# One chunk's direct term added by GpSimd, and the second block's first products recorded behind the first norm

## The chip, the core and the metric

The kernel runs on one core of a Trainium2 chip. A core has a matrix engine (PE, with PEld for its weight loads), a vector engine (DVE), a scalar engine (ACT), GpSimd (POOL) and a queue engine (SP) that issues most transfers. The metric is the time of one execution in microseconds, and lower is better. Three runs of the kernel before took 1164.25, 1165.2 and 1166.44 us, median 1165.2. The execution that the profiler recorded took 1164.2 us; its span from the first to the last instruction is 1162.0 us.

## The reference

Four layers follow each other on a signal of 2048 positions by 512 channels: a state-space convolution, a gated feed-forward network, and both again, each behind a layer norm and each added to its input.

```python
x = A_u
for _ in range(2):
    x = x + _A_ref(_layernorm(x), ...)   # y = irfft(rfft(u) * rfft(K)) + u * Dskip
    x = x + _B_ref(_layernorm(x), ...)   # (silu(x @ w_gate) * (x @ w_up)) @ w_down
```

K is a filter of 2048 taps for each channel, summed from 128 complex exponentials. The convolution is causal. Dskip, the direct term, multiplies the normed input; adding Dskip to the first tap of K has the same effect.

## The kernel before

The positions are cut into four blocks of 512 (`T`), and the convolution into products of block spectra. A block's output is the sum, over the blocks up to it, of an input spectrum times a filter spectrum. The channels are cut into eight chunks of 64 for the filter and into two halves (`h`) for the convolution; the spectra are cut into four quarters `q`, taken in the order 0, 3, 1, 2.

For each chunk the kernel makes the taps on PE (`lags`), spreads them over the partitions into `kt`, adds the direct term to the first tap (`skip`, L503) and turns `kt` into filter spectra on PE. For the last chunk the spreading goes through PE (`spread_pe`: matmuls L523, then one ACT copy L525 into `kt`). `first_parts` (L580) and `later_parts` (L531, with ACT copies L598 and L599 and a DVE addition L600 per quarter) make its spectra.

`ssm_half` convolves one half of one block. For each quarter it multiplies the input spectrum by the filter spectrum on DVE (L776, a tile `yk` of 128x1024); for an earlier block it loads a filter tile `w` and an input tile `uu`, multiplies (L776 into `t`) and adds (L779). Two DVE operations fold `yk` into `yf` (L781, L782), PE transforms it back (L796 into `pi`), and ACT or DVE combines the quarters (L748, L756, L757). After four quarters DVE combines them into the block's rows in two pieces (L811 to L815, then L820 to L825). The first block's two halves are the generators `conv[0]` and `conv[1]`; its input spectra and filter spectra are in SBUF, while each later block also needs loads.

The feed-forward weights are stored as pairs of 16-bit parts. `split_weights` loads them in pieces; ACT makes the high part (`hi`, L664 and L689) and DVE the low part (`lo`, L669 and L692). The scale of these splits comes from `scales()`, a run of small DVE operations (L344 to L356), so that no split can start before it. `first_norm` makes the norm of the first 256 rows for the feed-forward network: DVE statistics (L203 to L205), a power on POOL (L206), DVE L209, ACT rows L841, PE transposes L843, ACT L846 and DVE L848. `sizes` (ACT L607) and `direct_size` (ACT L192, DVE L193) bound the values for a later scale.

What sets the order: up to L1213 the instructions of ACT, DVE, PE and POOL stand as the code records them (`tc.manual_schedule`), and `take(generator, n)` records the next `n` steps of one part. SP and everything behind that block are ordered by a scheduler, which can also put later instructions into gaps of the recorded order. Each engine and each queue runs its instructions in order; an instruction that waits holds up all behind it.

The piece that the change touches, L1161 to L1212, runs from about 250 to 318 us of the span: the first block's convolution, the last chunk's spectra, the weight splits and the first norm, up to the first feed-forward matmul (`pgu`, L909, L910 and L912). From there on the feed-forward networks of the blocks alternate on PE with the convolutions of the next ones; `pgu` has two buffers, and each is freed by a DVE operation on it (L916).

Of the kernel before, what the change touches and what calls it, by code (L numbers as in the profile page):

```python
# [21 lines left out]
L, D, F = 2048, 512, 1376  # L22
# [22 lines left out]
SEQ = ((0, 0), (0, 1), (0, 2), (1, 0), (0, 3), (1, 1), (1, 2), (1, 3))  # L45
# [29 lines left out]
def kernel(ctx, tc, x, a_re, a_im, b_re, b_im, c_re, c_im, log_dt, d_skip,  # L75
                           w_gate, w_up, w_down, c_ef, c_ei, c_ek, c_am, c_eh, c_eih, out):
    nc = tc.nc
    V, A, G, PE = nc.vector, nc.scalar, nc.gpsimd, nc.tensor
# [9 lines left out]
    def tl(shape, name, tag, dt=F32):  # L88
        return sb.tile(shape, dt, name=name, tag=tag, bufs=BUFS[tag])
# [4 lines left out]
    def psml(shape, name):  # L94
        return ps.tile(shape, F32, name=name, tag="sml", bufs=4)
# [92 lines left out]

    def direct_size():

        da = tl([1, D], "da", "uu")
        A.activation(da, dsk, AF.Abs)  # L192
        V.tensor_reduce(dmax, da, axis=AX.X, op=OP.max)  # L193

# [32 lines left out]
    def stt(o, i0, s, i1, op1):  # L227
        V.scalar_tensor_tensor(o, i0, s, i1, OP.mult, op1)  # L228

    def load_x(xt, layer, b):  # L230
        if layer == 0:
            nc.sync.dma_start(xt, x[0, b * T:(b + 1) * T, :].rearrange("(c p) d -> p c d", p=P))
        else:
            nc.sync.dma_start(xt, xdr[b].rearrange("c p d -> p c d"))
# [5 lines left out]
    def whole(t):  # L240

        return t.rearrange("p i (c d) -> p i c d", c=NQ)
# [257 lines left out]
    def skip(ch, kt, eng):  # L500

        k = kt[0:1, :, 0]
        eng.tensor_tensor(k, k, dsk[:, ch * DC:(ch + 1) * DC].rearrange("p (g d) -> p g d", g=4), OP.add)  # L503
# [14 lines left out]
    def spread_pe(ks, kt):  # L518

        kp = pbig([P, 4, 16, 16], "kp")  # L520
        for grp in range(4):
            for ga in range(4):
                PE.matmul(kp[32 * ga:32 * ga + 32, grp], lhsT=ident[:, 32 * grp:32 * grp + 32], rhs=ks[:, ga],  # L523
                          start=True, stop=True, tile_position=(0, 32 * ga))
        A.activation(kt, kp, AF.Copy)  # L525
# [79 lines left out]
    def sizes(ch, kt, junk):  # L605

        A.activation(junk, kt, AF.Abs, accum_out=wsum[:, ch:ch + 1])  # L607
# [21 lines left out]
    def take(it, n):  # L629
        for _ in range(n):  # L630
            next(it, None)
# [99 lines left out]
    def ssm(layer, b):  # L731

        if (layer, b) == SEQ[INV]:
            nc.sync.dma_start(eih, c_eih)
        for h in range(2):
            yield from ssm_half(layer, b, h)

    def ssm_half(layer, b, h):
        first = layer == 0 and b == 0
        half = SEQ.index((layer, b)) >= INV  # L740
        hs = slice(h * HD, (h + 1) * HD)
        bb = {}

        def combine(q, pi):
            if q < 2:
                pair = tl([P, 2, 2, HD], "bb", "bd") if h == 0 or not first else bb1[:, q]
                bb[q], bb[q, 1] = pair[:, 0], pair[:, 1]
                A.activation(bb[q], pi, AF.Copy, scale=sy[:, 1:2] if half else 1.0)  # L748
                return
            s = bb[3 - q]  # L750
            bb[q] = bb[3 - q, 1]
            if half:
                stt(bb[q], pi, sy[:, 2:3], s, OP.add)
                stt(s, pi, sy[:, 1:2], s, OP.add)
            else:
                V.tensor_tensor(bb[q], s, pi, OP.subtract)  # L756
                V.tensor_tensor(s, s, pi, OP.add)  # L757

        late = []
        for _ in range(4):  # L760
            hq, q, u = ahead.pop(0)
            nxt = next(spec, None)
            if nxt:
                ahead.append(nxt)
            yk = tl([P, NQ, 2, 2, DC], "yk", "y1")
            y = yc if half else tl([P, 2, HD], "yf", "w")
            for k in range(b + 1):
                if k == 0:
                    w, uu = w0r[:, h, q], u
                else:  # L770
                    w = tl([P, NQ, 2, DC], "w", "w")
                    nc.sync.dma_start(w, wdr[k, h, q])
                    uu = tl([P, NQ, 2, DC], "uu", "uu")
                    nc.sync.dma_start(uu, udr[layer][b - k, h, q])
                t = tl([P, NQ, 2, 2, DC], "t", "t") if k else yk
                V.tensor_tensor(t, uu.unsqueeze(2).to_broadcast([P, NQ, 2, 2, DC]),  # L776
                                w.unsqueeze(3).to_broadcast([P, NQ, 2, 2, DC]), OP.mult)
                if k:
                    V.tensor_tensor(yk, yk, t, OP.add)  # L779
            yo = whole(y)  # L780
            V.tensor_tensor(yo[:, 0], yk[:, :, 0, 0], yk[:, :, 1, 1], OP.subtract)  # L781
            V.tensor_tensor(yo[:, 1], yk[:, :, 0, 1], yk[:, :, 1, 0], OP.add)  # L782
            if half:
                yl = yl2[:, QORD.index(q) % 2]
                A.activation(yl[:, 0], y, AF.Copy, scale=sy[:, 0:1])  # L785
                stt(yl[:, 1], y, sy[:, 0:1], yl[:, 0], OP.subtract)
            pi = psml([P, 2, HD], "pi")
            with tc.high_priority(offset=0 if first else BOOST):
                for o in range(2):
                    if half:  # L790
                        terms = [(eih[:, q, 0 if i == o else 1 + o, le], yl[:, ly, i])
                                 for i in range(2) for le, ly in ((0, 0), (0, 1), (1, 0))]
                    else:
                        terms = [(ei[:, q, 0 if i == o else 1 + o], y[:, i]) for i in range(2)]
                    for k, (e, m) in enumerate(terms):
                        PE.matmul(pi[:, o], lhsT=e, rhs=m, start=k == 0, stop=k == len(terms) - 1)  # L796
            late.append((q, pi))
            if first and q < 2 or len(late) > 1:
                combine(*late.pop(-1 if first and q < 2 else 0))
            yield  # L800
        for l in late:
            combine(*l)
        s03, e03, d03, f03 = bb[0][:, 0], bb[0][:, 1], bb[3][:, 0], bb[3][:, 1]
        s12, e12, d12, f12 = bb[1][:, 0], bb[1][:, 1], bb[2][:, 0], bb[2][:, 1]
        xt = xs[SEQ.index((layer, b)) % 3]
        if h == 0 and not first:
            load_x(xt, layer, b)
        o = [xt[:, c, hs] for c in range(4)]
        t1 = tl([P, HD], "t1", "t1")
        t2 = tl([P, HD], "t2", "t1")  # L810
        V.tensor_tensor(t1, s03, s12, OP.add)  # L811
        stt(t2, d12, TT, e12, OP.subtract)
        V.tensor_tensor(o[0], o[0], t1, OP.add)
        stt(t1, e03, -TT, d03, OP.add)
        V.tensor_tensor(t1, t1, t2, OP.add)  # L815
        stt(o[1], t1, CC, o[1], OP.add)
        yield
        t1 = tl([P, HD], "t1", "t1")
        t2 = tl([P, HD], "t2", "t1")
        V.tensor_tensor(s03, s03, s12, OP.subtract)  # L820
        V.tensor_tensor(f03, f03, f12, OP.add)
        stt(t2, d03, TT, e03, OP.subtract)
        stt(t1, e12, TT, d12, OP.subtract)
        V.tensor_tensor(s03, s03, f03, OP.subtract)
        V.tensor_tensor(t1, t1, t2, OP.add)  # L825
        stt(o[2], s03, HH, o[2], OP.add)
        stt(o[3], t1, CC, o[3], OP.add)
        yield
# [122 lines left out]
    with tc.manual_schedule(engines={mybir.EngineType.Activation, mybir.EngineType.DVE, mybir.EngineType.PE, mybir.EngineType.Pool}):  # L951
# [165 lines left out]
        c, kts, tail = NCH - 1, (kt2[:, 0], kt2[:, 1]), {}  # L1117
# [29 lines left out]
        load_x(xs[0], 0, 0)  # L1147
        split(0, 0, 3)
        conv = [ssm_half(0, 0, h) for h in range(2)]

        def slots():
# [9 lines left out]
        norm = first_norm(tl([P, 2, D], "nn1", "hf"))  # L1161
        take(conv[0], 1)
        spread_pe(ks, kts[1])
        skip(c, kts[1], V)
        take(conv[0], 1)
        scales()
        split(1, 0)
# [20 lines left out]
        split(0, 0, 1)  # L1188
        take(odd, 2)
        take(conv[1], 1)  # L1190
        take(norm, 1)
        take(rest, 2)
        take(odd, 1)
        take(norm, 1)
        take(rest, 1)
        take(odd, 2)
        split(1, 0)
# [10 lines left out]
        take(rest, 4)  # L1208
        split(0, 0, 3)
        sizes(c, kts[1], ks)  # L1210
        direct_size()
        nn2 = tl([P, 2, D], "nn2", "nn")  # L1212
        take(second(*sec[-1]), 2)  # L1213
    pscale = product_scale()
# [7 lines left out]
    xs[2] = tl([P, 4, D], "xf", "xf")  # L1222
    for i, lb in enumerate(SEQ):
        if i + 1 < len(SEQ):
            take(ssm(*SEQ[i + 1]), 100)
        if i == 0:
            take(pscale, 100)
        ffn(*lb, ready if i == 0 else None)
# [38 lines left out]
```

## Time and profile before

| what | us |
|---|---|
| median of three runs | 1165.2 |
| the profiled execution | 1164.2 |
| its span | 1162.0 |
| PE busy | 1100.7 (95%) |
| DVE busy | 998.6 (86%) |
| ACT busy | 598.7 (52%) |
| POOL busy | 107.9 (9%) |

The profile gives for each engine the instructions in order of time, each with the idle time of the engine ahead of it and what ended that wait. Shares over the whole span mix stages with different limits, so the stages are read one by one. Times of day below are microseconds from the start of the span.

### The profile page before, as it was taken

To read this page: it belongs to the slowest core of one execution; us is meant where nothing else is said; L and a number is where in the kernel's file an instruction comes from. 1 tells how busy PE (TensorE), PEld (TensorE's weight loads), DVE (VectorE), ACT (ScalarE), POOL (GpSimd) and SP (SyncE) were. 2 spreads that over 40 slices of the span, in tenths; PEclk is the share of its full clock that TensorE was granted. 3 is DMA by queue.
4 is the path that set the end of the run, shared out by engine and by line. 5 is a ranking of instruction groups with operands and counts; after the bars stand their busy time and mean duration, and the time that the engine had idled before them with its cause. 6 is when DMAs were issued, how large, how long until landed. Compare 5 with 4: busy or idle time off the path is not lost.

```text
span 1162.0 us, 24400 instructions
## 1 busy us (share of the span) xinstructions
PE 1100.7 (95%) x9942; PEld 877.9 (76%) x9942; DVE 998.6 (86%) x1586; ACT 598.7 (52%) x1198; POOL 107.9 (9%) x162
## 2 busy tenths in 40 slices
PE   2989999998889999999999999999999999999998
PEld 1868888877766868687868687868777686876875
DVE  8999999959789899999899999989994999983212
ACT  6989889733553353557453534655433452334211
POOL 0113222210000010010010000210000010000000
PEclk9989999998899999999999999999999999999999
DMA  5357777866383446332254544343534145312000
GB/s 208 131 161 164 169 175 187 197 171 218 122 268 122 132 122 219 101 115 73 79 155 140 126 162 141 105 128 93 158 109 150 48 122 145 115 42 46 15 23 19
DMA packets 127314, 150.38 MB, mean 129 GB/s; under 512 B 50897, under 2 KB 75985, under 8 KB 127202
## 3 DMA queue, kind: packets, MB, share of 16 engines
q1 hardware_dynamic: 115298, 123.32, 34.8%
q0 software_dynamic: 11904, 25.50, 9.5%
q8 instruction: 78, 1.28, 0.5%
q14 instruction: 34, 0.28, 0.1%
HBM read 98.70 MB, written 33.82 MB: 114 GB/s over the span
## 4 chain that ended last, share of the span: by engine, by line
PE 33%; DVE 27%; issue 7%; DMA 4%; ACT 3%; SPq 1%; POOL 1%; DVEq 0%; ACTq 0%; POOLq 0%
PE pgu L909 5%; PE pgu L910 5%; PE pgu L912 5%; DVE t L776 4%; PE py L924 4%; DVE yk L779 4%; PE py L925 4%; PE py L926 3%; DVE yk L776 3%; DVE z L228 2%; PE pi L796 2%; PE pf L280 2%; DVE sg L916 2%; DMA w<-wdr 2%; DMA mix<-nn 2%
## 5 line engine op out<-in xcount | busy, mean ns | idle before, releaser
L909 PE MATMUL pgu<-mix,wsl 128*128 128x256 f16 x1280 | 299.2, 273 | 5.0 <-DVE sg L916 5.0
L910 PE MATMUL pgu<-mix,wsl 128*128 128x256 f16 x1280 | 298.9, 273 | 0.0
L912 PE MATMUL pgu<-mix,wsl 128*128 128x256 f16 x1280 | 195.4, 273 | 0.0
L910 PEld LDWEIGHTS <-wsl 128*128 128x128 f16 x1280 | 125.4, 98 | 21.9 <-issue 5.4
L924 PE MATMUL py<-wsl,hh 128*128 128x512 f16 (+1 forms) x352 | 133.5, 379 | 6.3 <-DVE xg L929 4.2
L909 PEld LDWEIGHTS <-wsl 128*128 128x128 f16 x1280 | 125.4, 98 | 16.2
L912 PEld LDWEIGHTS <-wsl 128*128 128x128 f16 x1280 | 125.4, 98 | 14.9
L926 PE MATMUL py<-wsl,hl 128*128 128x512 f16 (+1 forms) x352 | 133.4, 379 | 1.2 <-DVE hl L918 1.1
L776 DVE TENSOR_TENSOR t<-uu,w 128x1024 f32<-128x1024 f32 x96 | 116.7, 1215 | 5.5 <-DMA w<-wdr 5.2
L925 PE MATMUL py<-wsl,hh 128*128 128x512 f16 x320 | 121.3, 379 | 0.0
L915 ACT ACTIVATE sg<-pgu,sc 128x512 f32<-128x512 f32 x80 | 54.6, 683 | 126.6 <-PE pgu L912 122.0
L779 DVE TENSOR_TENSOR yk<-yk,t 128x1024 f32<-128x1024 f32 x96 | 116.6, 1214 | 0.1
L916 DVE SCALAR_TENSOR_TENSOR sg<-pgu,sc,sg 128x512 f32<-128x512 f32 x80 | 59.4, 743 | 52.2 <-ACT sg L915 52.0
L917 ACT ACTIVATE hh<-sg 128x512 f16<-128x512 f32 x80 | 50.1, 626 | 82.3 <-DVE sg L916 82.3
L531 PE MATMUL pw<-kt,ek 128*128 128x256 f32 (+1 forms) x384 | 92.2, 377 | 0.0
L531 PEld LDWEIGHTS pw<-kt,ek 128*128 128x128 f32 x384 | 73.5, 196 | 8.7
L796 PE MATMUL pi<-yl,mix 128*128 128x256 f16 x576 | 78.9, 273 | 1.3 <-ACT yl L785 0.9
L280 PE MATMUL pf<-z,eh 128*128 128x256 f16 x576 | 74.9, 272 | 0.6 <-DVE z L228 0.6
L776 DVE TENSOR_TENSOR yk<-u,w0r 128x1024 f32<-128x1024 f32 x56 | 68.0, 1214 | 0.8 <-ACT u L282 0.8
L918 DVE TENSOR_TENSOR hl<-sg,hh 128x512 f16<-128x512 f32 x80 | 54.7, 683 | 15.5 <-ACT hh L917 15.5
L496 PE MATMUL pk<-re,g 128*32 128x64 f32 x1024 | 65.1, 317 | 2.6 <-DMA g<-g 1.9
L925 PEld LDWEIGHTS <-hh 128*128 128x128 f16 (+1 forms) x352 | 34.5, 98 | 42.5 <-issue 7.0
(237 smaller groups left out, 2160.5 us busy)
## 6 DMA issues: line engine op xcount, KB each, us to landing
w<-wdr SPq DMA_DIRECT2D x96, 256.0 KB, 2.8
uu<-udr SPq DMA_DIRECT2D x96, 256.0 KB, 3.0
udr<-u POOLq DMA_DIRECT2D x32, 256.0 KB, 2.6
g<-g POOLq DMA_DIRECT2D x6, 1024.0 KB, 9.1
udr<-u SPq DMA_DIRECT2D x16, 256.0 KB, 2.9
n<-xdr SPq DMA_DIRECT2D x4, 1024.0 KB, 5.7
kdr<-ks SPq DMA_DIRECT2D x6, 512.0 KB, 2.6
kt<-kdr SPq DMA_DIRECT2D x24, 128.0 KB, 3.0
```

Source lines behind the costliest of these rows:

```text
L280: PE.matmul(pf[:, o], lhsT=e, rhs=m, start=k == 0, stop=k == len(terms) - 1)
L531: PE.matmul(pw[:, i], lhsT=e, rhs=kt[:, :, c + 4 * k0:4 * k1:4, :].rearrange("p g k d -> p k g d"), start=c == 0, stop=c == 3)
L776: V.tensor_tensor(t, uu.unsqueeze(2).to_broadcast([P, NQ, 2, 2, DC]), w.unsqueeze(3).to_broadcast([P, NQ, 2, 2, DC]), OP.mult)
L779: V.tensor_tensor(yk, yk, t, OP.add)
L796: PE.matmul(pi[:, o], lhsT=e, rhs=m, start=k == 0, stop=k == len(terms) - 1)
L909: PE.matmul(o, lhsT=wgu(wi, k, 0)[:, fs], rhs=nh[:, k], start=k == 0, stop=False)
L910: PE.matmul(o, lhsT=wgu(wi, k, 1)[:, fs], rhs=nh[:, k], start=False, stop=False)
L912: PE.matmul(o, lhsT=wgu(wi, k, 0)[:, fs], rhs=nlo[:, k], start=False, stop=k == 3)
L916: V.scalar_tensor_tensor(sg, pgu[:, 1], sc6[:, 4:5], sg, OP.mult, OP.mult)
L924: PE.matmul(py[:, r], lhsT=hh[:n, f, rc], rhs=wd(f, 0)[:n], start=f == 0, stop=False)
L925: PE.matmul(py[:, r], lhsT=hh[:n, f, rc], rhs=wd(f, 1)[:n], start=False, stop=False)
L926: PE.matmul(py[:, r], lhsT=hl[:n, f, rc], rhs=wd(f, 0)[:n], start=False, stop=f == FT - 1)
```

## The change

Three edits. The last chunk's `skip` is given to GpSimd. The size of the direct term is recorded some steps earlier, with its tile in another pool. The first quarter of block 1 (its products, up to the folded `yf`) is recorded behind the second step of the first norm; for that `ssm_half` yields once more in that quarter, and the generator is finished where the whole of it stood.

```diff
-        da = tl([1, D], "da", "uu")
+        da = tl([1, D], "da", "sg")
...
-        for _ in range(4):
+        for s in range(4):
...
             V.tensor_tensor(yo[:, 1], yk[:, :, 0, 1], yk[:, :, 1, 0], OP.add)
+            if (layer, b, h, s) == (0, 1, 0, 0):
+                yield
...
-        skip(c, kts[1], V)
+        skip(c, kts[1], G)
...
         take(conv[1], 1)
+        direct_size()
+        block1 = ssm(0, 1)
         take(norm, 1)
         take(rest, 2)
         take(odd, 1)
         take(norm, 1)
+        take(block1, 1)
         take(rest, 1)
...
         sizes(c, kts[1], ks)
-        direct_size()
...
-            take(ssm(*SEQ[i + 1]), 100)
+            take(ssm(*SEQ[i + 1]) if i else block1, 100)
```

The lines behind the new ones move down in the changed kernel: L796 becomes L798, L820 becomes L822, L848 becomes L850, L909 becomes L911.

DVE ahead of and behind the last chunk's direct term, before (`kt` holds its taps, `yk` and `yf` are the first block's products):

```order
L776 TENSOR_TENSOR yk<-mix,w0r 128x1024
L781 TENSOR_TENSOR yf<-yk 128x256
L782 TENSOR_TENSOR yf<-yk 128x256
L503 TENSOR_TENSOR kt_429<-kt_429,tdk 1x4x16
L776 TENSOR_TENSOR yk<-mix,w0r 128x1024
L781 TENSOR_TENSOR yf<-yk 128x256
L782 TENSOR_TENSOR yf<-yk 128x256
L344 TENSOR_REDUCE c_2718<-cmx 128x3
```

On DVE L503 is gone and the rest stands as it stood. It now stands on POOL, behind the last accumulating stores of the filter and ahead of the first norm's power:

```order
L327 DMA st<-in_B_w_up_dram 128x344 x6
L538 DMA wdr<-wa 128x3x128 x2
L503 TENSOR_TENSOR kt_429<-kt_429,tdk 1x4x16
L206 TENSOR_TENSOR rs<-rs,mhalf 128x2
L223 TENSOR_TENSOR rs<-mv,mhalf 128x2
```

POOL has one instruction more there, and L206 comes behind it. DVE around the first norm, before:

```order
L205 TENSOR_SCALAR rs<-mv 128x2
L669 SCALAR_TENSOR_TENSOR wsl_2665<-st_2758,sc_92,wsl_2665 128x2x344
L669 SCALAR_TENSOR_TENSOR wsl_2666<-st_2758,sc_92,wsl_2665 128x2x344
L209 SCALAR_TENSOR_TENSOR rs<-mv,rs 128x2
L600 TENSOR_TENSOR wos<-pw,wos 128x2x3x64 x2
L600 TENSOR_TENSOR mix<-pw,mix 128x2x3x64
L848 TENSOR_TENSOR mix<-pt,mix 128x1024
```

The same place in the changed kernel:

```order
L209 SCALAR_TENSOR_TENSOR rs<-mv,rs 128x2
L600 TENSOR_TENSOR wos<-pw,wos 128x2x3x64
L776 TENSOR_TENSOR yk<-u,w0r 128x1024
L776 TENSOR_TENSOR t<-uu,w 128x1024
L779 TENSOR_TENSOR yk<-yk,t 128x1024
L781 TENSOR_TENSOR yf<-yk 128x256
L782 TENSOR_TENSOR yf<-yk 128x256
L600 TENSOR_TENSOR wos<-pw,wos 128x2x3x64
L776 TENSOR_TENSOR yk<-u,w0r 128x1024
L600 TENSOR_TENSOR mix<-pw,mix 128x2x3x64
L850 TENSOR_TENSOR mix<-pt,mix 128x1024
```

Block 1's first quarter has come in between the first two L600, and the scheduler has put the next quarter's first product between the second and the third. Before, the scheduler had put the first quarter's first product further ahead, between L756 and L757 of the first block's last half; that one is gone from there. PE ahead of the feed-forward network, in the changed kernel (`pf` is the last input spectrum, `pi` block 1's first back transform):

```order
L531 MATMUL pw<-kt_429,ek_84 128x192 x3
L296 MATMUL pf<-n_1626,ef 128x256
L798 MATMUL pi<-yf,mix 128x256 x4
L296 MATMUL pf<-n_1626,ek_84 128x256
L296 MATMUL pf<-n_1628,ek_84 128x256 x2
L296 MATMUL pf<-n_1626,ef 128x256
L296 MATMUL pf<-n_1626,ek_84 128x256
L296 MATMUL pf<-n_1628,ek_84 128x256 x2
L911 LDWEIGHTS wsl_2665
```

Before, no L796 stood here; block 1's first back transform came inside the third feed-forward tile.

## The prediction

> **What bounds the kernel now.** I first read the windows by stage: busy time of PE, PEld, DVE, ACT and POOL, then PE's granted clock.
>
> ```profile
> core 0: us, PE busy (x) PEld busy (x) DVE busy (x) ACT busy (x) POOL busy (x), PEclk, DMA share, GB/s
> 262.00:299.00 37.00, 28.34 (x152) 24.93 (x152) 35.74 (x68) 10.69 (x17) 1.35 (x1) 0.88 0.58 191
> 264.00:266.00 2.00, 2.00 (x6) 1.56 (x5) 1.79 (x11) 0.47 (x1) 0.00 (x0) 0.50 1.07 378
> 317.00:332.00 15.00, 10.45 (x96) 9.18 (x94) 13.93 (x23) 12.70 (x23) 0.70 (x1) 0.98 1.04 369
> 332.00:1162.00 830.00, 814.30 (x6785) 627.43 (x6783) 695.83 (x1153) 353.49 (x684) 52.97 (x68) 1.00 0.37 109
> ```
>
> Two stages with different limits. From 262 to 299 DVE works 35.74 of 37 us. From 332 to the end PE works 814.30 of 830 us: there the end of the kernel is the start of that stage plus PE's work plus at most 15.7 us of waits. So the change is worth what it moves PE's entry into that stage, plus the PE work that it takes out of the stage. Next the order of time on DVE (start, duration, idle time before it and what ended that).
>
> ```profile
> 251.74 0.42 DVE L782 TENSOR_TENSOR yf<-yk 128x256 f32<-128x256 f32 x1
> 261.63 0.21 DVE L503 TENSOR_TENSOR kt<-kt,tdk 1x64 f32<-1x64 f32 x1 [9.47 <-ACT kt L525]
> 261.78 1.20 DVE L776 TENSOR_TENSOR yk<-mix,w0r 128x1024 f32<-128x1024 f32 x1
> ...
> 267.28 1.77 DVE L669 SCALAR_TENSOR_TENSOR wsl<-st,sc,wsl 128x688 f16<-128x688 f32 x2
> ...
> 288.00 1.22 DVE L776 TENSOR_TENSOR yk<-u,w0r 128x1024 f32<-128x1024 f32 x1
> 289.14 0.68 DVE L757 TENSOR_TENSOR bb<-bb,pi 128x512 f32<-128x512 f32 x1
> ...
> 298.64 0.15 DVE L209 SCALAR_TENSOR_TENSOR rs<-mv,rs 128x2 f32<-128x2 f32 x1
> 298.71 0.55 DVE L600 TENSOR_TENSOR wos<-pw,wos 128x384 f32<-128x384 f32 x1
> 303.39 0.56 DVE L600 TENSOR_TENSOR wos<-pw,wos 128x384 f32<-128x384 f32 x1 [4.12 <-ACT wos L599]
> 306.13 0.56 DVE L600 TENSOR_TENSOR mix<-pw,mix 128x384 f32<-128x384 f32 x1 [2.19 <-ACT mix L599]
> ```
>
> DVE stands idle 9.47 us at the last chunk's direct term, in front of the stage that it bounds, and then 4.12 and 2.19 us behind the norm. The same stretch on PE:
>
> ```profile
> 258.58 1.93 PE L523 MATMUL kp<-ks,ident 128*32 128x256 f32 x32
> 263.50 3.43 PE L796 MATMUL pi<-yf,mix 128*128 128x256 f32 x8 [2.98 <-DVE yf L781]
> ...
> 268.50 1.95 PE L796 MATMUL pi<-yf,mix 128*128 128x256 f32 x8
> ...
> 283.51 5.69 PE L796 MATMUL pi<-yf,mix 128*128 128x256 f32 x16 [2.53 <-DVE yf L781]
> ...
> 316.57 0.27 PE L909 MATMUL pgu<-mix,wsl 128*128 128x256 f16 x1
> 316.68 0.27 PE L910 MATMUL pgu<-mix,wsl 128*128 128x256 f16 x1
> ...
> 326.61 0.60 PE L912 MATMUL pgu<-mix,wsl 128*128 128x256 f16 x4
> 331.76 0.37 PE L909 MATMUL pgu<-mix,wsl 128*128 128x256 f16 x1 [4.55 <-DVE sg L916]
> 331.92 0.42 PE L910 MATMUL pgu<-mix,wsl 128*128 128x256 f16 x1
> 332.13 0.42 PE L909 MATMUL pgu<-mix,wsl 128*128 128x256 f16 x1
> ```
>
> PE waits for DVE's folded products at 263.50 and 283.51, and after two feed-forward tiles for DVE's L916. The gate at 331.76 is the entry that I follow. Two pieces of the chain that ended last (start, duration), one ahead of the gate and one behind it:
>
> ```profile
> 315.02 5.24 DMA st<-in_B_w_down_dram
> ...
> 332.53 5.90 DMA w<-wdr
> ```
>
> Ahead of the 5.24 us load of `w_down` that chain runs through the spectra on PE, the norm and DVE's row of work from 283.8 us on; the load starts when the last spectra's buffers are free. So a microsecond gained on DVE before 299 arrives at 331.76, unless something else is late.
>
> **The direct term on GpSimd.** DVE is free at 251.74 + 0.42 = 252.16 and goes on with L776. From there to L669 it has 267.28 - 261.78 = 5.50 us of work, so it would be there at 257.66. But L669 needs ACT's high part:
>
> ```profile
> 260.58 1.02 ACT L525 ACTIVATE kt<-kp 128x1024 f32<-128x1024 f32 x1 [1.30 <-PE kp L523]
> 265.52 1.44 ACT L664 ACTIVATE wsl<-st,sc 128x1376 f16<-128x1376 f32 x1 [3.92 <-DVE sc L356]
> ```
>
> L664 waited 3.92 us for the scale from DVE; that wait falls away, but L664 still stands behind L525, which ends at 260.58 + 1.02 = 261.60. L664 then ends at 261.60 + 1.44 = 263.04, and L669 starts at about 263.1 in place of 267.28: **4.2 us earlier**. The 9.47 us are not won whole; some 5.4 us of them become a wait for ACT.
>
> PE must not be later than that. It finishes L523 at 258.58 + 1.93 = 260.51, finds `yf` ready, and does the back transform in 1.95 us (the row at 268.50) instead of the 3.43 us that it took after its idle time: free at 262.46, in place of 266.93. Its next step, L580, now waits for POOL's addition, which cannot start before 261.60. The trace has no addition on POOL; the nearest row is its power on two or four columns (count: shortest/median/longest ns):
>
> ```profile
> L223 POOL TENSOR_TENSOR rs<-mv,mhalf x21: 697/1220/4027, 318.9 to 1056.4; 128x2 f32<-128x2 f32 x15, 128x4 f32<-128x4 f32 x6
> ```
>
> The lower bound is the 0.21 us of DVE's own L503, the upper one 4.03 us. Up to 0.86 us (262.46 - 261.60) it is hidden behind PE's back transform, and what exceeds this eats into the 2.53 us that PE waits at 283.51. I take 0.70 us, the shortest of these rows, since DVE is idle then: cost 0. At 4.03 us the loss is 4.03 - 0.86 - 2.53, about 0.6 us.
>
> **The moved direct size.** L193 leaves the place where ACT's splits hid it and stands ahead of the norm's statistics, where DVE is the bound; ACT's L192 comes 25 us ahead, where ACT has idle time.
>
> ```profile
> L193 DVE TENSOR_REDUCE dmax<-da x1: 665/665/665, 319.4 to 319.4; 1x1 f32<-1x512 f32 x1
> ```
>
> It **costs about 0.6 us** on the path; 0.67 at most.
>
> **Block 1's first quarter.** The product that the scheduler had put at 288.00 leaves DVE's full stretch: L757 starts 1.14 us after it, so **1.1 us won** there. Together L209 comes 4.2 + 1.1 - 0.6 = 4.7 us earlier, at 293.9. Behind it stand now three operations of 128x1024 at 1.22 us (like the row at 288.00) and two of 128x256 at 0.42 (like that at 251.74), 4.5 us, ahead of the L600 that had 4.12 us of idle time: 0.4 us late. The next quarter's product, 1.2 us, fits into the 2.19. So the moved 5.7 us lie in 6.3 us of idle time, and I count nothing for them. If that cover were gone, because PE and ACT come sooner, the cost would be up to the 4.5. The loads for it are ahead: `w` was issued at 286.29 in the trace and nothing in front of it in SP's queue gets later; `uu` comes from a store made long before.
>
> ```profile
> 286.29 0.34 SPq L772 DMA_DIRECT2D w<-wdr  x1
> ```
>
> On PE the back transform adds 1.95 us ahead of the network and is taken out of the third tile. So the first tile starts at 316.57 - 4.7 + 1.95 = 313.8, and the second ends at 327.21 - 4.7 + 1.95 = 324.5. Between, ACT and DVE keep their order of splits in front of L916, with one quarter's `t` and addition there as before. So L916 frees the buffer 4.7 us earlier, and the third tile starts at 331.76 - 4.7 = 327.1. PE's wait there shrinks from 4.55 to about 2.6 us, because the back transform is done inside it.
>
> **The sum.** The third tile comes 4.7 us earlier with 1.95 us of PE work less behind it: 6.65 us. DVE also has 3.3 us less behind it (`t`, addition, folds), so it does not fall behind a PE that has 1.95 less. I take nothing for it: with PE waiting at most 15.7 us in 830, the gain would be about 2 us, and the reordered rest may cost as much. Span 1162.0 - 6.65 = 1155.35; the execution is 2.2 us longer than its span, 1157.6; the median of the runs shown lies 1.0 above the profiled one: **1158.6 us**.
>
> One rule bears on the remaining wait. After the idle 2.98 us at 263.50 the granted clock was 0.50 (264 to 266), and after the 4.55 us at 331.76 matmuls start 0.21 us apart (331.92 and 332.13) against 0.11 at 316.57. The Trainium skill (TensorE: Matmul & The Clock Gate, Part 1: The HAM clock gate) says that the array falls to half clock after an idle window of about 3.4 us; by this a wait of 2.6 us might pass without it, and the sum would be 1.5 us less, 1157.1. The row at 263.50 speaks against it, since 2.98 us were enough, so the sum stays.
>
> **The rivals.** (1) *The hole is too small*: PE and ACT deliver the spectra before DVE is through with block 1's quarter, and DVE's later work (the rows of the first block, which free a buffer for `w_down`) slips. For it: 5.7 us into 6.3 is tight. Against it: the additions L600 free buffers that PE wants only several microseconds later. 2 to 4.3 us of the 4.5 are lost: 1160.6 to 1162.9. (2) *The wait only moves*: PE at L580, or ACT, holds DVE as long as L503 did, since L525 still ends at 261.60 and POOL's spans reach 4.03 us. That needs POOL to take 4.2 + 0.86 + 2.53, some 7.6 us; then the other edits' 1.1 - 0.6 + 1.95 = 2.4 us are left, or nothing: 1162.8 to 1165.2. The Trainium skill (Perfetto Trace Analysis, Optimizing Scalar/DVE Operations) warns that GpSimd shares a read port with DVE, so that moving work between the two might not help; at 261.60 DVE is waiting, so here it would hardly apply. (3) *Slower*: `t` now stands in DVE's recorded order ahead of every L600, the norm's second part and the splits, and waits for `w` and `uu`. If the load of `w` slips behind others (one took 5.90 us in the chain above), everything behind it stops. It loses from the point where `w` lands 6.65 us after `t`'s turn at about 295.7 (293.9 and the L600 and L776 behind it), so after 302; a load issued at 302 and taking 5.9 would give 5.7 us more than before, 1171. Against it: issued at 286.29 it has 9 us.
>
> **How the numbers follow.** Forecast 0.70 (1156 to 1160.6), rival 1 0.13, rival 2 0.10, rival 3 0.07. A measurement of this kernel can tell about 0.2%, 2.3 us, from no change: faster means below 1162.9, slower above 1167.5. Faster takes the forecast and nearly all of rival 1: 0.82; same, most of rival 2: 0.11; slower, rival 3: 0.07. The range runs from 1155.5, with the better 2 us of the rest and another microsecond from the clock, to 1163.0, the end of rival 1; it leaves out rivals 2 and 3.
>
> **What would show it.** Right: no DVE wait at L503; L669 at about 263.1; L209 near 294; the idle times behind it filled by L776, L779, L781 and L782; the first tile near 313.8 and the third near 327.1. Wrong: a POOL span at L503 above 3 us with PE waiting at L580, a wait of DVE for `w` near 296, or PE's waits behind 332 growing beyond 15.7 us; the last would say that the entry was not what sets the end.

## The result and the profile after

The changed kernel is faster: 1154.0 to 1156.5 us in three executions against 1164.25 to 1166.44 before, a ratio of 0.9909 with a 95% interval of 0.9895 to 0.9924. Two disturbed executions, one here (2880.89 us) and one of experiment 6 (1289.36 us), are left out. In five more rounds it took 1155.22 us (median) against 1163.99 before, ratio 0.9922 (0.9907 to 0.9937). The forecast was 1158.6, so 3 to 4 us more were gained than it said. The profiled execution took 1156.48 us; its span is 1154.7.

The same stages in the windows of the changed kernel (length; busy time of PE, PEld, DVE, ACT, POOL; PE's clock; DMA share; GB/s):

```profile
262.00:299.00 37.00, 29.31 (x162) 26.49 (x161) 34.60 (x56) 14.06 (x25) 1.65 (x2) 0.87 0.62 208
317.00:332.00 15.00, 11.68 (x96) 9.80 (x95) 14.45 (x22) 12.75 (x20) 0.00 (x0) 0.89 0.96 319
332.00:1154.70 822.70, 808.37 (x6754) 622.90 (x6752) 687.90 (x1142) 351.28 (x679) 54.00 (x68) 1.00 0.36 108
```

Nothing has changed its limit: DVE still fills the first window and PE the last. What moved shows in the order of time on DVE:

```profile
258.13 0.42 DVE L782 TENSOR_TENSOR yf<-yk 128x256 f32<-128x256 f32 x1
263.34 1.78 DVE L669 SCALAR_TENSOR_TENSOR wsl<-st,sc,wsl 128x688 f16<-128x688 f32 x2 [4.79 <-ACT wsl L664]
...
290.19 0.67 DVE L193 TENSOR_REDUCE dmax<-da 1x1 f32<-1x512 f32 x1
...
294.28 0.15 DVE L209 SCALAR_TENSOR_TENSOR rs<-mv,rs 128x2 f32<-128x2 f32 x1
294.35 0.55 DVE L600 TENSOR_TENSOR wos<-pw,wos 128x384 f32<-128x384 f32 x1
294.81 1.21 DVE L776 TENSOR_TENSOR yk<-u,w0r 128x1024 f32<-128x1024 f32 x1
...
299.14 0.55 DVE L600 TENSOR_TENSOR wos<-pw,wos 128x384 f32<-128x384 f32 x1
299.60 1.22 DVE L776 TENSOR_TENSOR yk<-u,w0r 128x1024 f32<-128x1024 f32 x1
301.94 0.56 DVE L600 TENSOR_TENSOR mix<-pw,mix 128x384 f32<-128x384 f32 x1 [1.12 <-ACT mix L599]
```

The wait of 9.47 us for `kt` is gone, and 4.79 us of it have become a wait for ACT's high part. The idle times of 4.12 and 2.19 us behind the norm are filled with block 1's products, up to 1.12 us. On POOL, and then on PE:

```profile
262.07 0.31 POOL L503 TENSOR_TENSOR kt<-kt,tdk 1x64 f32<-1x64 f32 x1 [17.29 <-ACT kt L525]
```

```profile
260.82 1.99 PE L798 MATMUL pi<-yf,mix 128*128 128x256 f32 x8
...
279.60 3.61 PE L798 MATMUL pi<-yf,mix 128*128 128x256 f32 x8 [2.73 <-DVE yf L781]
...
309.35 1.89 PE L798 MATMUL pi<-yf,mix 128*128 128x256 f32 x8
...
314.10 0.27 PE L911 MATMUL pgu<-mix,wsl 128*128 128x256 f16 x1
...
328.06 0.37 PE L911 MATMUL pgu<-mix,wsl 128*128 128x256 f16 x1 [3.32 <-DVE sg L918]
```

The addition takes 0.31 us on POOL, and PE does not wait for it. The first feed-forward tile starts at 314.10 (forecast 313.8). The third starts at 328.06 (forecast 327.1, before 331.76). This start is called the gate below. Ahead of it PE waits 3.32 us, as against 4.55.

### The profile page after: what moved, and what is told of

It reads as the page before. It is cut to its first block, busy times and chain, and to the rows that moved or that the text cites. A ratio compares the mean times of both kernels' runs of the same rounds, so it can differ in the third digit from the quotient of the medians.

```text
span 1154.7 us, 24400 instructions
## 1 busy us (share of the span) xinstructions
PE 1100.2 (95%) x9942; PEld 877.6 (76%) x9942; DVE 998.7 (86%) x1585; ACT 599.1 (52%) x1198; POOL 109.5 (9%) x163
## 4 chain that ended last, share of the span: by engine, by line
PE 35%; DVE 23%; issue 8%; DMA 5%; ACT 3%; SPq 1%; POOL 1%; DVEq 0%; ACTq 0%; POOLq 0%
PE pgu L911 6%; PE pgu L912 6%; PE pgu L914 6%; PE py L926 4%; PE py L927 3%; PE py L928 3%; DVE t L776 3%; DVE yk L779 3%; PE pi L798 2%; PE pf L280 2%; DMA w<-wdr 2%; DVE yk L776 2%; DVE z L228 2%; DVE sg L918 1%; DMA mix<-nn 1%
## 5 line engine op out<-in xcount | busy, mean ns | idle before, releaser
L911 PE MATMUL pgu<-mix,wsl 128*128 128x256 f16 x1280 | 299.0, 273 | 4.3 <-DVE sg L918 3.3
L911 PEld LDWEIGHTS <-wsl 128*128 128x128 f16 x1280 | 125.3, 98 | 16.1
L779 DVE TENSOR_TENSOR yk<-yk,t 128x1024 f32<-128x1024 f32 x96 | 116.8, 1216 | 0.2
L798 PE MATMUL pi<-yl,mix 128*128 128x256 f16 x576 | 78.9, 272 | 0.6 <-DVE yl L228 0.3
L496 PE MATMUL pk<-re,g 128*32 128x64 f32 x1024 | 65.1, 317 | 2.4 <-DMA g<-g 2.4
```

Source lines behind the costliest of these rows:

```text
L911: PE.matmul(o, lhsT=wgu(wi, k, 0)[:, fs], rhs=nh[:, k], start=k == 0, stop=False)
```

## The experiments

The first four ran together with the kernel before, in five rounds. Each kernel has two readings: the time against the kernel before, and, in its one profiled execution, the gate and what lies behind it up to the end of the span. The table after the last experiment has both for all.

**1. The changed kernel once more.**

> The changed kernel once more, to settle how much of its gain belongs to every execution. Theory T1 (the terms add up to 6.65 us, in the profiled pair 7.3 us of span, and the rest of the 10 us between the medians is scatter from execution to execution): over five rounds the median gain is 7 to 8.5 us, ratio 0.9927 to 0.994. Rival T2 (every execution gains some 3 us more than the terms, by work that the profiled execution of the changed kernel lost again): the median gain is 10 to 11 us again, ratio 0.9905 to 0.9915, and the execution profiled here is about 1154, with a span near 1152.

Measured: 1155.22 against 1163.99 us, 8.8 less. The gate is at 327.12 and the span 1153.4. This is just above what T1 allowed and well below T2, and the profiled execution does not lie 3 us from the medians either. So the gain of the first comparison, with four executions of the kernel before, was 1 to 2 us too large by scatter. A true 8.8 us is still 2.1 us more than the 6.65 of the terms. The windows from the gate on, before and in this execution (PE's busy time is the first number behind the length):

```profile
331.76:500.00 168.24, 162.85 (x1324) 124.89 (x1324) 159.93 (x268) 73.23 (x145) 11.90 (x17) 0.99 0.47 145
500.00:840.00 340.00, 337.00 (x2868) 264.65 (x2866) 327.21 (x562) 176.73 (x347) 31.41 (x38) 1.00 0.41 122
840.00:1162.00 322.00, 314.70 (x2598) 238.07 (x2596) 208.94 (x325) 103.76 (x193) 9.67 (x13) 1.00 0.26 77
```

```profile
327.12:500.00 172.88, 170.36 (x1394) 131.57 (x1394) 164.16 (x281) 76.38 (x149) 13.30 (x18) 0.98 0.47 141
500.00:840.00 340.00, 336.62 (x2864) 264.05 (x2862) 327.49 (x559) 176.22 (x346) 30.96 (x37) 1.00 0.40 122
840.00:1153.40 313.40, 306.59 (x2525) 230.72 (x2522) 200.28 (x310) 101.26 (x189) 9.64 (x13) 1.00 0.26 76
```

Subtract PE's busy time from the length and its waits remain: 5.39 + 3.00 + 7.30 = 15.7 us before, 2.52 + 3.38 + 6.81 = 12.7 now. Nearly all of the difference lies ahead of 500 us.

**2. The direct term alone.** The kernel before with one edit:

```diff
-        skip(c, kts[1], V)
+        skip(c, kts[1], G)
```

> The kernel before with the direct term's addition given to GpSimd and nothing else. T1: the low part L669 starts 4.2 us earlier (about 263.1), the third feed-forward tile about 4.2 us earlier (327.6), and the time is 4 to 5 us less, 1160.5. Rival R1 (the wait only moves, or the work behind takes the gain back because PE and ACT are no earlier): 0 to 2 us less. T2: 6 us or more less, if the additional 3 us come from this edit, since it also takes away a cold start of PE.

Measured: 1166.53 us, ratio 1.0017 (1.0004 to 1.0030): no gain, rather a loss. All three theories missed the time, while T1 was right on the front: L669 starts at 263.11, and the gate comes 5.7 us earlier, more than the 4.2 forecast; DVE's two waits for L599 behind the norm have shrunk too, to 3.51 and 1.40 us. The rest gives it back. The profiled execution took 1162.24 us and is the fastest of twelve, so it shows only a part of the loss: 4 us behind the gate, where the 5.7 us of the gate and the median together lack about 8. The windows say where those 4 lie:

```profile
326.03:500.00 173.97, 168.94 (x1370) 130.09 (x1370) 165.19 (x279) 76.39 (x149) 12.33 (x18) 0.98 0.49 145
500.00:840.00 340.00, 333.82 (x2833) 261.04 (x2832) 323.85 (x555) 176.78 (x343) 27.99 (x37) 1.00 0.40 121
```

Between 500 and 840 us PE waits 6.2 us in place of 3.0. The waits of PE there, total, times and longest:

```profile
PE py L924 <- DVE xf L929: 2.8, 2, 2.3
PE py L924 <- DVE xg L929: 1.4, 1, 1.4
PE pi L796 <- ACT yl L785: 1.0, 2, 0.5
```

No edit touches that stretch. But the scheduler had ordered it anew: set against the kernel before, PE's order of 14985 rows differs in 1232 (those gone and those new, counted together; the expectations below count them so too), spread over the whole rest: the traces of the two differ up to 868 us. For the changed kernel they differ only up to about 420 us.

**3. The products alone.** The changed kernel with the direct term back on DVE. PE's and ACT's orders are then those of the changed kernel in every row.

```diff
-        skip(c, kts[1], G)
+        skip(c, kts[1], V)
```

> The changed kernel with the direct term's addition put back on DVE: only the products of block 1 behind the norm, and the size of the direct term moved. T1: +1.1 (the product at 288.00 gone) -0.6 (L193 ahead of the norm) +1.95 (PE's back transform out of the third tile) = 2.4 us less than before, up to 3.5 with shorter waits of PE behind the gate; 1162. Rival R2 (the moved 5.7 us do not fit into DVE's idle time when the hole is where it was): 0 or slower. T2: 5 us or more less, if the additional 3 us come from here.

Measured: 1159.79 us, 4.2 less than before; ratio 0.9965 (0.9952 to 0.9977). This is between T1 and T2. Against experiment 1, which differs from it in the direct term alone, the direct term is worth 4.6 us, where 4.2 were forecast. The products are worth 4.2, where 2.4 were. Two of its rows, DVE and PE:

```profile
261.22 0.21 DVE L503 TENSOR_TENSOR kt<-kt,tdk 1x64 f32<-1x64 f32 x1 [9.52 <-ACT kt L525]
```

```profile
330.59 0.27 PE L911 MATMUL pgu<-mix,wsl 128*128 128x256 f16 x1 [2.94 <-DVE sg L918]
```

The wait of DVE is back, and the gate is 1.2 us earlier than before; the larger part of the gain comes behind it.

**4. The high part first.** In the changed kernel the spreading matmuls (now `spread_mm`, which returns `kp`) and the copy into `kt` are parted, and the scale's steps and the high part stand between them.

```diff
-        spread_pe(ks, kts[1])
-        skip(c, kts[1], G)
-        take(conv[0], 1)
+        kp = spread_mm(ks)
         scales()
         split(1, 0)
+        A.activation(kts[1], kp, AF.Copy)
+        skip(c, kts[1], G)
+        take(conv[0], 1)
```

> The changed kernel with ACT's order turned round at the last chunk: the scale's matmul and the high part L664 (1.44 us) recorded between the spreading matmuls and the copy into kt, so that the high part runs while PE still spreads. T1 says that DVE bounds 262 to 299 and waits there 4.8 us for this high part: L669 comes 1.5 to 2 us earlier, kt about 0.2 us later, and the time is 1.5 to 2 us less than the changed kernel's. Rival R3 (behind L669 PE or ACT is the bound, so that an earlier L669 brings nothing): within 0.5 us of the changed kernel, with a new DVE wait for ACT or PE between 265 and 294.

Measured: 1154.16 us, ratio 0.9911 (0.9895 to 0.9927). The lines are four further down in this kernel:

```profile
260.66 1.78 DVE L673 SCALAR_TENSOR_TENSOR wsl<-st,sc,wsl 128x688 f16<-128x688 f32 x2 [2.79 <-ACT wsl L668]
...
268.72 1.23 DVE L780 TENSOR_TENSOR yk<-mix,w0r 128x1024 f32<-128x1024 f32 x1 [0.90 <-ACT w0r L585]
```

```profile
325.51 0.37 PE L915 MATMUL pgu<-mix,wsl 128*128 128x256 f16 x1 [3.03 <-DVE sg L922]
```

The low part starts 2.6 us earlier than in experiment 1 (263.25), 0.9 of it are lost again in a wait for the filter spectra, and the gate is 1.6 us earlier. T1 holds for the rows. In the times it is 1.1 us less than the changed kernel, within their scatter: the intervals overlap.

**5 and 6. The same front, two orders behind it.** Experiment 2 with small DVE additions that nobody reads, six or twelve. They change what the scheduler counts on, and with twelve it orders the rest almost as in the kernel before.

```diff
-        skip(c, kts[1], V)
+        scr = tl([1, 4, 16], "scr", "sg")
+        for _ in range(6):
+            V.tensor_tensor(scr, ..., ..., OP.add)
+        skip(c, kts[1], G)
```

> The direct term alone on GpSimd, as in the second experiment, with six small DVE additions (1x64, into a scratch tile that nobody reads) where DVE's own addition stood; they lie in front of the 5.1 us that DVE waits for the high part L664 there, so they cost nothing. The scheduler then still orders the rest behind the recorded block as it did for that experiment (PE's order is the same in all 14985 rows; 1232 stand elsewhere than in the kernel before). Theory T3 (the edit itself gains about 5.5 us up to the third feed-forward tile, and the order that the scheduler made behind it loses that again between 600 and 780 us): time as the second experiment's, 1164 to 1168, third tile at about 326, loss behind 600. Rival T4 (the gain is lost for another reason, whatever the order): the same here, and the same with twelve additions.

> The same with twelve of the small additions, about 2.4 us of DVE time that lie in front of its wait. With these the scheduler orders the rest as in the kernel before, up to 66 of PE's 14985 rows, all of them ahead of 500 us. T3: the third tile at about 326 again, and now nothing is lost behind it: 5 to 6 us less than before, 1158 to 1159.5, some 7 us less than with six additions. T4: as with six additions, 1164 to 1168.

Measured: 1164.71 us with six (ratio 1.0007, 0.9992 to 1.0022) and 1159.12 with twelve (0.9961, 0.9948 to 0.9973). T3 holds in the times, T4 falls. The front with twelve was not the expected one: the scratch tile's buffer had to wait for a store, and twelve additions were more than DVE's wait could hide.

```profile
255.80 2.94 DVE L1166 TENSOR_TENSOR scr<-tdk 1x64 f32<-1x64 f32 x12 [2.40 <-DMA wdr<-wo]
```

With twelve, the gate comes 2.7 us later than with six (329.46 and 326.77), and the kernel is still 5.6 us faster. Behind the gate it is 6.5 us shorter (829.0 and 835.5), with 14.3 us of PE's waits in place of 19.2.

**7. The size in DVE's wait.** Experiment 4 with the size ahead of the spreading matmuls.

```diff
+        direct_size()
         kp = spread_mm(ks)
...
-        direct_size()
         block1 = ssm(0, 1)
```

> The kernel with the high part in front of the copy into kt (the fourth experiment), and besides the size of the direct term recorded ahead of the spreading matmuls, so that L193 (0.67 us) leaves DVE's full stretch ahead of the norm and lies where DVE waits 2.8 us for the high part, and ACT's L192 where ACT waits 7.7 us for PE. By my terms 0.6 to 0.7 us less than the fourth experiment (1153.5), 8.7 + 1.0 + 0.6 = 10.3 us less than before. Rival (the norm's start is not what the gate follows): within 0.2 us of it. The two can be told apart in the traces by the start of the norm's L209 and of the third tile; the times alone scatter by more.

Measured: 1158.36 us against 1164.38, 6.0 less, where experiment 4 had 9.8. Both expectations missed. The rows on DVE and ACT (of its slowest execution, 1163.87 us):

```profile
259.75 0.68 DVE L193 TENSOR_REDUCE dmax<-da 1x1 f32<-1x512 f32 x1 [7.70 <-ACT da L192]
```

```profile
256.81 1.02 ACT L507 ACTIVATE ks<-pk 128x1024 f32<-128x1024 f32 x1 [7.71 <-PE pk L497]
258.61 0.60 ACT L752 ACTIVATE bb<-pi 128x512 f32<-128x512 f32 x1 [0.78 <-PE pi L802]
259.11 0.61 ACT L192 ACTIVATE da<-tdk 1x512 f32<-1x512 f32 x1
```

L192 stood in ACT's queue behind L507, which waits 7.71 us for PE, and DVE's scale stood behind L193. So the high part waited for the scale, and the low part L673 started at 265.99 in place of 260.66. An instruction put into one engine's idle time held up another's chain. The gate is 6.7 us later than in experiment 4; the median lost only 3.8, so a usual execution may have lost less there.

**8. Another order alone.** The kernel before with one small addition on GpSimd ahead of DVE's own.

```diff
+        scr = tl([1, 4, 16], "scr", "sg")
+        G.tensor_tensor(scr, kts[1][0:1, :, 0], ..., OP.add)
         skip(c, kts[1], V)
```

> The kernel before with one small addition on GpSimd (1x64, from kt into a scratch tile that nobody reads) ahead of DVE's own: nothing else changes up to 318 us but that DVE's addition comes some 0.3 to 0.5 us later. The scheduler makes another order of the rest of it (782 of PE's 14985 rows stand elsewhere). T3 (the order behind the block is worth several us by chance): a time that differs from before by 1.5 us or more in one direction, with the difference arising behind 480 us. T4 (the order there is worth less than 1 us): 0.3 to 0.8 us slower than before.

Measured: 1162.3 us, 2.1 less than before (1164.38); ratio 0.9981 (0.9967 to 0.9994). The gate is at 331.94, 0.2 us later than before, and behind it lie 828.7 us in place of 830.2. T3 in size, but not in place: the lead is there at 373 us already (4.4 us in DVE's L929 rows), and 1.3 to 2 us of it are left from 438 us on. Of the orders tried, the one before is neither the best nor the worst.

**9 and 10. GpSimd late.** The changed kernel with 10 and 26 more additions ahead of the direct term:

```diff
+        scr = tl([1, 4, 16], "scr", "sg")
+        for _ in range(10):
+            G.tensor_tensor(scr, kts[1][0:1, :, 0], ..., OP.add)
         skip(c, kts[1], G)
```

> The changed kernel with ten more additions on GpSimd (1x64, from kt into a scratch tile that nobody reads) ahead of the direct term; no instruction of PE, DVE, ACT or SP stands elsewhere. At 0.31 us each kt is complete 3.1 us later. By my prediction's reckoning (0.86 us behind PE's back transform and 2.53 us of PE's wait) that is hidden: within 0.5 us of the changed kernel. Rival T5 (the next to be late is not PE's wait at 279.5 but DVE's product that reads the filter spectra copied by L581; that copy ends 1.8 us ahead of it, and PE had 0.27 us): 3.1 - 0.27 - 1.8, about 1 us slower, with a wait of DVE for ACT's w0r near 271.

> The same with 26 more additions, 8.1 us. By my prediction's reckoning 8.1 - 0.86 - 2.53 = 4.7 us slower than the changed kernel, about what the edit gained; T5: 8.1 - 0.27 - 1.8 = 6.0 us slower, of which the wait of DVE for w0r shows 6. Rival: 26 additions take another time than 26 times one (a fixed start of GpSimd paid once): then the delay on POOL is to be read first and both sums made with it.

Measured: 1163.01 us (ratio 1.0002, 0.9993 to 1.0011) and 1169.08 us (1.0048, 1.0035 to 1.0060). All sums were too small. First the delay: on POOL in experiment 1, then with ten, then with 26.

```profile
261.98 0.31 POOL L503 TENSOR_TENSOR kt<-kt,tdk 1x64 f32<-1x64 f32 x1 [17.29 <-ACT kt L525]
```

```profile
261.14 5.92 POOL L1168 TENSOR_TENSOR scr<-kt,tdk 1x64 f32<-1x64 f32 x10 [17.29 <-ACT kt L525]
267.14 0.31 POOL L503 TENSOR_TENSOR kt<-kt,tdk 1x64 f32<-1x64 f32 x1
```

```profile
261.80 12.10 POOL L1168 TENSOR_TENSOR scr<-kt,tdk 1x64 f32<-1x64 f32 x26 [17.29 <-ACT kt L525]
273.98 0.31 POOL L503 TENSOR_TENSOR kt<-kt,tdk 1x64 f32<-1x64 f32 x1
```

The delays are 6.0 and 12.2 us, not 3.1 and 8.1. Most additions start 0.39 us apart; five that ran beside DVE's L669, its next product and the folds took 0.38 to 1.18 us each, which adds 2.1 us to both delays (see the last section). Counted from the start of POOL's first addition, the gate comes 7.7 and 13.6 us later than in experiment 1 (72.9 and 78.7 against 65.1 us): the whole delay and 1.5 us more. With the delay of 6.0 the reckoning of the prediction gives 6.0 - 0.86 - 2.53 = 2.6 us, T5 gives 3.9. T5 named the right wait, on DVE with ten additions:

```profile
271.52 1.23 DVE L776 TENSOR_TENSOR yk<-mix,w0r 128x1024 f32<-128x1024 f32 x1 [3.70 <-ACT w0r L581]
...
277.14 1.23 DVE L776 TENSOR_TENSOR yk<-mix,w0r 128x1024 f32<-128x1024 f32 x1 [3.59 <-ACT w0r L581]
```

There are two such waits, 7.3 us together. Both sums left out that PE goes cold (half clock, granted 0.50 from 266 to 274 us) while it waits:

```profile
267.50 1.11 PE L580 MATMUL pw<-kt,ef 128*128 128x64 f32 x4 [5.61 <-POOL kt L503]
...
270.97 3.73 PE L798 MATMUL pi<-yf,mix 128*128 128x256 f32 x8
```

In experiment 1 the same two groups take 0.55 and 1.95 us.

**11. The size behind the norm.** The changed kernel with the size recorded after the norm's first step.

```diff
-        direct_size()
         block1 = ssm(0, 1)
         take(norm, 1)
+        direct_size()
```

> The changed kernel with the size of the direct term recorded one step later, so that L193 stands behind the norm's L209 instead of ahead of its statistics; nothing else moves. By my terms L209 comes 0.6 us earlier (293.6 instead of 294.2) and the time falls by 0 to 0.6 us, since DVE then has the 0.6 us more in the stretch behind L209, where about 0.5 us of idle time were left. Rival (the gate follows ACT and PE behind the norm): the whole 0.6 us. Either is smaller than the scatter of the times; the rows decide.

Measured: 1154.39 us against 1163.12, 8.7 less, as experiment 1. Counted from the start of POOL's addition, L209 comes 0.56 us earlier than there (292.89 - 261.24 against 294.19 - 261.98), as forecast, and the gate 0.5 us later. The 0.6 us are thus won at the norm and lost again behind it, as the terms allowed and the rival did not.

**12. The size in two halves.** Experiment 4 with ACT's half behind the copy into `kt` and DVE's behind the first low part. The reason given in the expectation for the wait in experiment 7 is wrong: it was ACT's order, not the buffer.

```diff
         A.activation(da, dsk, AF.Abs)
+        yield
         V.tensor_reduce(dmax, da, axis=AX.X, op=OP.max)
...
         skip(c, kts[1], G)
+        size = direct_size()
+        take(size, 1)
...
         first_parts(c - 1, 3)
+        take(size, 1)
...
-        direct_size()
         block1 = ssm(0, 1)
```

> The kernel with the high part in front of the copy into kt (fourth experiment), with the two halves of the size apart: ACT's L192 behind the copy into kt, where ACT waits 3.1 us for PE, and DVE's L193 behind the first low part L669, 6 us ahead of a place where DVE waits 0.90 us for the filter spectra. The tile's buffer was not free at 256 us (a wait of 7.70 us of DVE in the seventh experiment); at 262 us it is. By my terms L209 and the third tile come 0.6 us earlier than in the fourth experiment (292.5 and 325.5) and the time is 0.6 us less, about 1153.6. Rival (DVE's wait for the filter spectra grows by as much): no change.

Measured: 1153.78 us against 1163.12, ratio 0.9919 (0.9906 to 0.9933). The gate is at 324.95, 0.56 us earlier than in experiment 4, and the wait for the filter spectra shrank from 0.90 to 0.44 us, as the terms said. At 826 us in the trace the lead over experiment 4 has gone to 0.04 us: PE's waits behind the gate are 15.1 us in place of 13.2. In the times, experiments 4 and 12 cannot be told from each other or, for certain, from the changed kernel.

All of them. "Less" is the median of before in the same comparison minus the kernel's median; the last three columns are from the profiled execution, "behind" from the gate to the span's end.

| kernel | less, us | gate | behind | PE's waits behind |
|---|---|---|---|---|
| before | | 331.76 | 830.2 | 15.7 |
| changed, first comparison | | 328.06 | 826.6 | 14.3 |
| 1 changed, again | 8.8 | 327.12 | 826.3 | 12.7 |
| 2 direct term alone | -2.5 | 326.03 | 834.3 | 18.1 |
| 3 products alone | 4.2 | 330.59 | 826.4 | 15.0 |
| 4 high part first | 9.8 | 325.51 | 826.6 | 13.2 |
| 5 direct term, six additions | -0.3 | 326.77 | 835.5 | 19.2 |
| 6 direct term, twelve | 5.3 | 329.46 | 829.0 | 14.3 |
| 7 size in the wait | 6.0 | 332.20 | 829.8 | 16.8 |
| 8 another order alone | 2.1 | 331.94 | 828.7 | 14.5 |
| 9 GpSimd late by 6.0 | 0.1 | 333.99 | 826.3 | 12.8 |
| 10 GpSimd late by 12.2 | -6.0 | 340.52 | 825.4 | 11.9 |
| 11 size behind the norm | 8.7 | 326.89 | 825.3 | 13.1 |
| 12 size in two halves | 9.3 | 324.95 | 827.1 | 15.1 |

Two of the profiled executions are not typical of their kernel: that of experiment 2 is its fastest (1162.24 us, median 1166.53) and that of experiment 7 its slowest (1163.87, median 1158.36).

## Why the prediction was right, and where it was wrong

**What bounds the kernel: right.** DVE's row of work ahead of the norm sets the gate, and PE most of the rest (the first 35 us behind the gate are looked at below). In experiments 2, 4 and 12 an earlier L669 gave an earlier gate, and in 9 and 10 a later product of DVE a later one.

**The direct term: right.** L669 at 263.34 (forecast 263.1), with the rest of the wait turned into one for ACT. Experiment 3 against 1 gives 4.6 us for a forecast of 4.2. The 0.70 us taken for GpSimd were 0.31.

**The size and block 1's quarter: right.** L209 at 294.28 (forecast 293.9), the size worth 0.56 us there (experiment 11), the holes filled, no wait of DVE for `w` in front of L779, the first tile within 0.3 us. The gate came 3.7 us earlier in the profiled execution and 4.64 in experiment 1; 4.7 were forecast.

**The step that failed: "I take nothing for it".** Behind the gate I counted only the 1.95 us of PE work that had moved ahead. I wrote that shorter waits of PE could bring about 2 us more and that the reordered rest might cost as much, and put zero. Measured in experiment 1: 830.24 - 826.28 = 3.96 us, that is 2.0 us beyond the 1.95. PE's waits are 2.99 us shorter (15.70 and 12.71). Its busy time is only 0.97 us shorter, since PE worked at half clock for about 5.7 us behind the gate, where it was about 2.9 before. Of the nine executions with the changed kernel's order behind the gate (its own two, experiments 3, 4, 7 and 9 to 12), eight lie within 825.3 and 827.1 us there, and one, experiment 7 in its slowest execution, at 829.8.

The accounts for 1158.6 - 1155.2 = 3.4 us close so: 2.0 behind the gate; 1.0 that I added because the median lay above the profiled execution, where over 18 executions it did not (1163.99 against 1164.2, and 1155.22 against 1155.21 for the changed kernel); 0.4 because the execution now lasts 1.8 us longer than its span and not 2.2. The gate itself was off by 0.1. The range went down to 1155.5 by allowing those 2 us and one more for the clock. The clock gave nothing in this execution (a matmul of 0.37 us at the gate). What went past the lower end is the 1.0 and the 0.4 of the step from span to median, and 0.7 by which the first comparison (1154.52) lies below experiment 1.

**Why the rest was worth 2 us: located, and not taken apart.** The fifth `hl<-sg,hh` of DVE behind the gate starts at 366.81 before, at 359.27 in experiment 1 and at 364.68 in experiment 6. From the gate to this row DVE does the same instructions in all three, except that experiment 1 has five of block 1's fewer. The windows from the gate to this row, in that order:

```profile
331.76:366.81 35.05, 34.14 (x264) 26.91 (x264) 31.46 (x48) 8.37 (x14) 0.41 (x2) 0.96 0.55 157
327.12:359.27 32.15, 32.15 (x245) 25.38 (x245) 27.22 (x43) 7.77 (x13) 0.41 (x2) 0.91 0.59 144
329.46:364.68 35.22, 34.81 (x273) 27.34 (x272) 31.50 (x48) 8.37 (x14) 0.41 (x2) 0.96 0.57 158
```

Before, PE (34.14 us busy of 35.05) stood idle for 0.91 us in this stretch, most of it in one wait for DVE's folds; in experiment 1 it does not wait at all. DVE (31.46 and 27.22) has 4.2 us less to do and not the 3.3 of the prediction, since the next quarter's first product has gone ahead of the gate too.

```profile
348.43 0.70 PE L796 MATMUL pi<-yf,mix 128*128 128x256 f32 x2 [0.72 <-DVE yf L781]
```

So 2.90 us are won by this row, 0.95 beyond the 1.95. In the nine executions it is 2.2 to 3.7 us, and in experiment 6, which keeps block 1's products where they stood, -0.2. Up to the eleventh such row (448.83 before) experiment 1 wins 0.4 us more, experiment 6 1.5. The last 0.7 of experiment 1 come behind that. So about half of the 2 us arose where the first quarter had stood. PE alone does not set this stretch: in experiments 3 and 7 it ran at full clock from the gate on, and then waited 1.7 and 1.8 us there, and the row came no sooner (2.7 and 2.2 us won). That points at DVE, whose lesser work I had put at nothing. Experiments 6 and 8 show that an order alone can be worth 1.2 to 1.6 us, not that it was worth this here. No run separates what DVE's lesser work did from what the new places of PE's back transforms did. The order can also cost more than it gives: in experiments 2 and 5 the stretch behind the gate is 4 to 5 us longer, and with it all that the direct term had won is gone.

**The rivals.** (1), the hole too small, did not come: 1.12 us of it were left over. (2), the wait only moves, did not come at 0.31 us. But its price was wrong: I had it need some 7.6 us on POOL, and experiment 9 shows that 6.0 us undo the whole gain of all three edits. I had counted PE's wait at 283.51 as slack. DVE's product that reads the copied filter spectra comes first, and a PE that waits 5.61 us then works at half speed. The shared port that the Trainium skill warns of (Perfetto Trace Analysis, Optimizing Scalar/DVE Operations) did not bear on the change itself, since DVE was waiting while the addition ran. The traces agree with the warning where both work: the same addition took 0.91 and 0.90 us in experiments 4 and 12, beside DVE's low part, and with ten additions on POOL DVE's L669 took 1.84 us as against 1.78. (3), `t` waiting for `w`, did not come: `t` ran at 295.95 without a wait.

**The clock.** I let the row at 263.50 speak: a wait of 2.98 us makes PE cold, so the 3.32 us at the gate did too (its matmul takes 0.37 us). That was right for this execution, and no rule: see the last section.

## What to carry to other kernels

Price an edit in two parts, up to the point where a scheduler takes over and behind it: an edit that leaves the order behind that point alone can be added up, and one that does not can lose all it won in a stretch that it never touched. Before a part is measured alone, compare the orders; if they differ, hold the order (here with additions that lie mostly in a wait) or measure the part by taking it out of the full change. An order can also be worth a microsecond or two by itself. An instruction moved into one engine's idle time brings along the queue in which its producer stands, so read that queue too.

## What the runs showed of the hardware

Whether a wait makes PE cold is not decided by its length here. Two executions of the changed kernel have the same wait in the same place, first in the first comparison, then in experiment 1:

```profile
279.60 3.61 PE L798 MATMUL pi<-yf,mix 128*128 128x256 f32 x8 [2.73 <-DVE yf L781]
```

```profile
279.50 1.99 PE L798 MATMUL pi<-yf,mix 128*128 128x256 f32 x8 [2.73 <-DVE yf L781]
```

The granted clock from 280 to 282 us was 0.50 in the one and 1.00 in the other. At the gate, 2.94 us in experiment 3 left PE at speed (a matmul of 0.27 us), and 2.98 us in experiment 12 did not (0.37 us), while the same 2.98 us in experiment 7 did (0.27 us):

```profile
324.95 0.37 PE L916 MATMUL pgu<-mix,wsl 128*128 128x256 f16 x1 [2.98 <-DVE sg L923]
```

The Trainium skill (TensorE: Matmul & The Clock Gate, Part 1: The HAM clock gate) says that the activity window runs freely, so that the point of change varies with where the work falls in it; the traces agree with that. Its figure of an idle window of about 3.4 us is not a lower bound for a wait: 2.73 us were enough once, and 2.53 in the kernel before (283.51, granted 0.50 from 284 to 286 us).

A small GpSimd addition takes longer while DVE works. In experiments 9 and 10 each one that ran while DVE was idle took 0.31 us, with 0.39 us from start to start. Those beside DVE's L669 and its next product (both read two tiles) took 0.83, 0.83 and 1.18 us in both experiments, and two beside the folds 0.45 and 0.38. The product took 1.33 us there, as against 1.22 in experiment 1. So ten took 5.92 us where 3.9 would be ten distances of 0.39. In experiment 12 the low part ran on DVE when the direct term's turn came:

```profile
260.57 1.78 DVE L674 SCALAR_TENSOR_TENSOR wsl<-st,sc,wsl 128x688 f16<-128x688 f32 x2 [2.75 <-ACT wsl L669]
```

```profile
261.62 0.90 POOL L504 TENSOR_TENSOR kt<-kt,tdk 1x64 f32<-1x64 f32 x1 [17.29 <-ACT kt L1173]
```

The Trainium skill (Perfetto Trace Analysis, GPSIMD Engine Instruction) advises to time such instructions by the distance of their starts and not by their spans. Here the one span of 0.31 us had made the delay of ten look like 3.1 us where it was 6.0.
